# Splits moved to VectorE, block sums kept in PSUM, and a planned distance ahead of matmuls, in a planner-ordered attention and MoE kernel

## The chip, the cores and the metric

The kernel runs on one core of one Trainium2 chip. The metric is the device time of the whole program in microseconds, from one launch. Every engine (TensorE, VectorE, ScalarE, GpSimd, and SyncE, which issues the DMAs) works through its own list of instructions in the order in which the program wrote them, and waits on semaphores where an instruction needs another engine's result.

## What is computed

Attention over 16 heads (2 batches of 8, 768 rows of 64 numbers), in which a query sees only the keys of its own hash bucket, and two feed-forward stages behind it:

```python
mask = q_bucket[:, :, :, None] == k_bucket[:, :, None, :]
scores = np.where(mask, scale * np.matmul(q, k.transpose(0, 1, 3, 2)), -1e9)
attn = softmax(scores)
x = np.matmul(attn, v)          # as 1536 tokens of 512
...
h = x @ w_in                    # 512 -> 2048
x = (h / (1 + np.exp(-h))) @ w_out
...
a, b = x @ w1, x @ w2           # 512 -> 1024 each
out = ((a * b) @ w3) @ w_out
```

## The kernel before

**The planner.** The program's order isn't written by hand. Each step is an `op` with the engines that could do it and its cost in ns on each, the ops it needs, a due time, and the buffers it takes and gives back. `Plan.run` walks a modelled clock: an op is ready when the ops it needs have ended by its costs, each engine takes the op that could start soonest, and among equals the one due first. The order so found is the order of the instructions on each engine. On the chip only the order counts, not the modelled time. The costs are `dve(n)`, `act(n)`, `pool1(n)`, `pool2(n)`, plus a `TAIL` for each engine. A VectorE op with `port=True` is never planned beside a GpSimd op.

**Split numbers.** Matmuls run on rounded fp32 (`F32R`). So that nothing is lost, each operand is held as a high part (rounded, a copy) and a low part (`sub`, L251: the value less its high part), and each product is three matmuls: high by high, high by low, low by high. Whoever makes a new operand therefore makes two instructions, one copy and one subtraction.

**Stages.** Attention runs from 0 to about 325 us of the trace, in 96 units of 128 query rows: scores (L615), their maximum, exp, transposes (L655), a split of the transposed weights (`pth` on ScalarE, `ptl` on VectorE), and products with V (L688). `move` takes a group's result out of PSUM with two copies. Beside it the two last weight matrices are multiplied into one (L751). Behind it come the two feed-forward stages in cells: (1, c, ...) is chunk c of the first, (2, c, ...) of the second, each a rise (L913, L1020), a gate, and falls (L1064). A fall's PSUM result is added to `X` on VectorE (L1081).

**Weights.** `piece` brings in 128 by 1024 weights in two halves. The host passes them as 64-bit words. One half goes: DMA into one of three `raw` buffers (L273), two ScalarE (or GpSimd) reads (L290, L294 or L298), a join and a sign step on VectorE (L304, L309; the second frees `raw`), then the high part (`hi`, L248 on GpSimd) and the low part (`lo`). With `duo=True` four sums of the weight blocks are made on GpSimd (L373), and split too (`hi_sum`, `lo_sum`).

**Pair cells.** Two of the three token blocks are computed together as a 2 by 2 block product with seven block products instead of eight. `rise_pair` runs the `CHAIN` one, five, six, two, seven, four, three over three PSUM banks p, q, r. Bank p is added to in steps one, six, seven, four; between these steps ScalarE copies (`snap`) the intermediate value to an `sg` buffer, so that the first matmuls of six, seven and four wait for a copy. `plus` then adds a bank to such a copy on VectorE (L929) and gives the four blocks. `gated` or `gate`/`meet` make the activation from a block, and `rounded` splits it into `gh` and `gl`. The buffers `qraw`, `kraw`, `qhi`, `qlo`, `khi`, `klo` of the attention are lent to this stage as further `sg`, `gh` and `gl`. `split` and `less` (L853) split and subtract the blocks of X between the stages. PSUM has two banks `acc` and, behind the attention, six more, `more`.

## Time and profile before

| | |
|---|---|
| three runs | 776.03, 781.65, 782.9 us; median 781.65 us |
| profiled execution | 779.35 us |
| its span in the trace | 777.6 us, mean granted TensorE clock 0.986 |
| TensorE matmuls | busy 742.4 us, 95% |
| VectorE | busy 582.8 us, 75%, 1050 instructions |
| ScalarE | busy 440.9 us, 57%, 853 instructions |
| GpSimd | busy 466.7 us, 60%, 434 instructions |

The profiled execution is one of its own, and its span is 1.75 us shorter than its time. A busy share is a mean over stages with different limits, so the stages are read one by one. Busy times of matmuls overlap, so a busy TensorE may still be slower than its best; in the trace three matmuls of 512 columns in a row take 0.68 us.

### The profile page before, as it was taken

To read this page: it belongs to the slowest core of one execution; us is meant where nothing else is said; L and a number is where in the kernel's file an instruction comes from. 1 tells how busy PE (TensorE), PEld (TensorE's weight loads), DVE (VectorE), ACT (ScalarE), POOL (GpSimd) and SP (SyncE) were. 2 spreads that over 40 slices of the span, in tenths; PEclk is the share of its full clock that TensorE was granted. 3 is DMA by queue.
4 is the path that set the end of the run, shared out by engine and by line. 5 is a ranking of instruction groups with operands and counts; after the bars stand their busy time and mean duration, and the time that the engine had idled before them with its cause. 6 is when DMAs were issued, how large, how long until landed. Compare 5 with 4: busy or idle time off the path is not lost. (4 is left out here: it accounts for less than half of the span.)

```text
span 777.6 us, 11071 instructions
## 1 busy us (share of the span) xinstructions
PE 742.4 (95%) x3727; PEld 630.5 (81%) x3727; DVE 582.8 (75%) x1050; ACT 440.9 (57%) x853; POOL 466.7 (60%) x434
## 2 busy tenths in 40 slices
PE   6898999999999999899999998999999999999998
PEld 6887898989888989687788876878787788888886
DVE  4997899999999998694887788769568643745245
ACT  4778799787787777574655364524543544313110
POOL 3365988968675554627667576658495385827000
PEclk7999999999999999999999999999999999999999
DMA  7496868776564541400304223120301111200003
GB/s 206 134 228 167 217 149 207 188 193 167 146 177 110 163 120 38 133 1 28 102 7 136 80 83 101 35 82 19 117 1 36 59 41 54 83 1 0 1 14 149
DMA packets 27593, 77.25 MB, mean 99 GB/s; under 512 B 4424, under 2 KB 4520, under 8 KB 27536
## 3 DMA queue, kind: packets, MB, share of 16 engines
q1 hardware_dynamic: 27536, 76.55, 35.1%
q8 instruction: 29, 0.48, 0.3%
q14 instruction: 28, 0.23, 0.1%
HBM read 52.44 MB, written 5.29 MB: 74 GB/s over the span
## 5 line engine op out<-in xcount | busy, mean ns | idle before, releaser
L913 PE MATMUL more<-y,piece 128*128 128x512 f32 x504 | 135.6, 396 | 9.6 <-ACT sg L244 4.6
L913 PEld LDWEIGHTS more<-y,piece 128*128 128x128 f32 x504 | 94.8, 190 | 33.4 <-ACT sg L244 6.4
L251 DVE TENSOR_TENSOR ptl<-turn,pth 128x384 fp32r<-128x384 f32 x192 | 101.6, 548 | 11.8 <-ACT pth L244 10.8
L637 ACT ACTIVATE P<-score,st 128x768 f32<-128x768 f32 x96 | 95.4, 993 | 19.1 <-DVE st L631 18.8
L244 ACT ACTIVATE pth<-turn 128x384 fp32r<-128x384 f32 x192 | 88.1, 487 | 26.7 <-PE turn L655 26.2
L621 DVE TENSOR_REDUCE st<-score 128x1 f32<-128x768 f32 x96 | 90.8, 948 | 10.2 <-PE score L615 9.7
L655 PE MATMUL turn<-ident,P 128*128 128x128 f32 x576 | 87.5, 277 | 5.9 <-DVE ptl L251 5.4
L655 PEld LDWEIGHTS turn<-ident,P 128*128 128x128 f32 x576 | 68.4, 141 | 21.5 <-DVE ptl L251 14.0
L1081 DVE SCALAR_TENSOR_TENSOR X<-more,X 128x512 f32<-128x512 f32 x87 | 58.2, 685 | 25.4 <-PE more L1064 25.3
L251 POOL TENSOR_TENSOR piece<-x,piece 128x512 fp32r<-128x512 f32 x52 | 72.4, 1395 | 2.5 <-ACT piece L244 1.3
L688 PE MATMUL acc<-pth,V 128*128 128x384 f32 x192 | 67.7, 353 | 0.4 <-ACT pth L244 0.4
L688 PE MATMUL acc<-ptl,V 128*128 128x384 f32 x192 | 64.8, 338 | 0.2 <-DVE ptl L251 0.2
L248 POOL TENSOR_SCALAR piece<-x 128x512 fp32r<-128x512 f32 x50 | 36.5, 734 | 46.1 <-PE acc L1064 17.7
L1064 PE MATMUL more<-gh,piece 128*128 128x512 f32 x170 | 63.3, 389 | 0.0
L703 POOL TENSOR_TENSOR X<-X,xt 64x384 f32<-64x384 f32 x32 | 33.1, 1034 | 46.5 <-DVE X L246 22.0
L615 PE MATMUL score<-ka,qa 128*128 128x384 f32 x192 | 55.3, 369 | 3.8 <-ACT P L637 3.5
L294 ACT ACTIVATE t<-raw 128x512 uint32<-128x512 uint32 x49 | 32.9, 674 | 43.7 <-DVE x L309 10.2
L751 PE MATMUL acc<-piece,piece 128*128 128x512 f32 x192 | 55.2, 407 | 0.0
L1020 PE MATMUL more<-xh,piece 128*128 128x512 f32 x160 | 51.2, 389 | 0.0
L251 POOL TENSOR_TENSOR piece<-sum,piece 128x512 fp32r<-128x512 f32 x30 | 43.4, 1457 | 12.9 <-ACT piece L244 12.2
L615 PE MATMUL score<-kb,qb 76*128 76x384 f32 x192 | 50.0, 342 | 0.0
L244 ACT ACTIVATE sg<-more 128x512 f32<-128x512 f32 x28 | 16.7, 596 | 47.8 <-PE more L913 44.8
(225 smaller groups left out, 1859.5 us busy)
## 6 DMA issues: line engine op xcount, KB each, us to landing
raw<-in_w SPq DMA_DIRECT2D x32, 512.0 KB
raw<-in_wo SPq DMA_DIRECT2D x24, 512.0 KB
raw<-in_win SPq DMA_DIRECT2D x16, 512.0 KB
ka<-khi SPq DMA_DIRECT2D x30, 192.0 KB
qraw<-in_qT SPq DMA_DIRECT2D x8, 384.0 KB
kraw<-in_kT SPq DMA_DIRECT2D x8, 384.0 KB
vraw<-in_v SPq DMA_DIRECT2D x8, 384.0 KB
invb<-inverse SPq DMA_DIRECT2D x16, 192.0 KB
```

What stands on the lines that cost most here:

```text
L244: nc.scalar.activation(out=dst, in_=src, func=AF.Copy, scale=by)
L251: engine[e].tensor_tensor(out=dst, in0=src, in1=hi.bitcast(F32), op=ALU.subtract)
L615: nc.tensor.matmul(out=sc[:, g, :HF], lhsT=lhs[:k, qs], rhs=rhs[:k, g * HF:g * HF + HF], start=(k == 128), stop=(k != 128),)
L621: nc.vector.tensor_reduce(out=plan[uk("st")][:, 0:1], in_=plan[uk("S")][:, :, :HF], op=ALU.max, axis=AX.XY, negate=True)
L637: nc.scalar.activation(out=plan[uk("P")], in_=plan[uk("S")][:, :, :HF], func=AF.Exp, scale=s[:, 1:2], bias=s[:, 2:3], accum_out=plan[hk("s ...
L655: nc.tensor.transpose(pt[:, c * 128:c * 128 + 128], P[:, g, c * 128:c * 128 + 128], ident)
L688: nc.tensor.matmul(out=xo[:, :N], lhsT=V[:, c, :], rhs=plan[gk(x)][:, c, :], start=(c == 0 and x == "pth"), stop=(c == NQ - 1 and x == "ptl"),
L751: nc.tensor.matmul(out=plan[key + ("ps",)], lhsT=w[:, a, k], rhs=r[:, c], start=(k == 0 and n == 0), stop=(k == 7 and n == 2),)
L913: nc.tensor.matmul(out=plan[bk[b]], lhsT=w[:, a], rhs=y, start=(opens and j == 0 and m == 0), stop=(j == 1 and m == 2), skip_group_check=True)
L1020: nc.tensor.matmul(out=plan[key], lhsT=w[:, a], rhs=x, start=(k == 0 and n == 0), stop=(k == 3 and n == 2))
L1064: nc.tensor.matmul(out=plan[key], lhsT=a, rhs=x, start=(f == 0 and n == 0), stop=(f == 1 and n == 2))
L1081: nc.vector.scalar_tensor_tensor(out=dst, in0=plan[key], scalar=by, in1=dst, op0=ALU.mult, op1=ALU.add)
```

## The change

It has three parts.

- **Engines.** For weights needed later than 20 us before the planned end of the attention (`behind`), the low part is made on VectorE alone and the high part on ScalarE or GpSimd; until now both were GpSimd's. The low parts of the weight sums, of X (`split`), of the activations (`rounded`), and the differences `less` and the product `meet` are VectorE's alone; until now GpSimd could take them.
- **Block sums.** `plus` writes some sums back to the PSUM bank they came from (`back`), frees the `sg` copy instead of the bank, and the gate reads the bank. In stage 1 these are the blocks of q and r, in stage 2 that of r.
- **Planner.** An op of ScalarE, VectorE or GpSimd that a matmul waits for counts as ended 250 ns later, and from 325 us of the planned clock on 1000 ns later (`SLACK`, `SLACK_FFN`). The costs of `move` and `invert` are raised.

The instruction counts that follow: VectorE has 111 such steps more and 12 copies fewer, GpSimd 151 instructions fewer, ScalarE 42 high parts of weights and 12 copies more. TensorE has the same matmuls.

```diff
+SLACK, SLACK_FFN, FFN_AT = 250.0, 1000.0, 325.0
...
-                h.ready = max(h.ready, at + ns if e == "PE" and "PE" in h.on else o.end)
+                late = (SLACK if at < 1000.0 * FFN_AT else SLACK_FFN) if e in ("ACT", "DVE", "POOL") and "PE" in h.on else 0.0
+                h.ready = max(h.ready, at + ns if e == "PE" and "PE" in h.on else o.end + late)
...
-            soon = need < BEGIN + SOON
-            h = op({"POOL": pool1(STEP), "ACT": act(STEP)} if soon else {"POOL": pool1(STEP)}, hi, [j, opener], due + 3, take=first)
+            soon, behind = need < BEGIN + SOON, need >= T_END - 20
+            h = op({"POOL": pool1(STEP), "ACT": act(STEP)} if soon or behind else {"POOL": pool1(STEP)}, hi, [j, opener], due + 3, take=first)
...
-            done.append(op({"POOL": pool2(STEP), "DVE": dve(STEP)} if soon else {"POOL": pool2(STEP)}, lo, [h], due + 4,
+            done.append(op({"DVE": dve(STEP)} if behind else {"POOL": pool2(STEP), "DVE": dve(STEP)} if soon else {"POOL": pool2(STEP)}, lo, [h], due + 4,
...
-            more_done.append(op({"POOL": pool2(STEP)}, lo_sum, [h], due + 1.5 + n / 1e3, give=[tmp + (n,)], port=True))
+            more_done.append(op({"DVE": dve(STEP)}, lo_sum, [h], due + 1.5 + n / 1e3, give=[tmp + (n,)], port=True))
...
-                mv = op({"ACT": 2 * act(N), "DVE": 2 * dve(N)}, move, [xo], tu + 3.5, [("xt", gk("xt"))], [gk("xo")])
+                mv = op({"ACT": 1005, "DVE": 1050}, move, [xo], tu + 3.5, [("xt", gk("xt"))], [gk("xo")])
...
-            iv = op({"DVE": 250}, invert, exps, te + 3)
+            iv = op({"DVE": 430}, invert, exps, te + 3)
...
-        return op({"DVE": dve(BLK), "POOL": pool2(BLK)}, low, [a], due + 0.5, port=True)
+        return op({"DVE": dve(BLK)}, low, [a], due + 0.5, port=True)
...
-            return op({"DVE": dve(BLK), "POOL": pool2(BLK)}, fold, deps, due, port=True)
+            return op({"DVE": dve(BLK)}, fold, deps, due, port=True)
...
-    def rise_pair(key, bank, of, due):
+    def rise_pair(key, bank, of, due, back):
...
-            def plus(dst, src, after, give=()):
+            def plus(dst, src, after, give=(), back=False):
...
-                    nc.vector.tensor_tensor(out=plan[u[dst]], in0=plan[bk[src]], in1=plan[u[dst]], op=ALU.add)
+                    nc.vector.tensor_tensor(out=plan[bk[src] if back else u[dst]], in0=plan[bk[src]], in1=plan[u[dst]], op=ALU.add)
...
-                return op({"DVE": dve(BLK)}, add, after, d, give=give)
+                return op({"DVE": dve(BLK)}, add, after, d, give=[u[dst]] if back else give)
...
-                c11 = plus("x", "q", [last, marks["x"]], freed("q"))
+                c11 = plus("x", "q", [last, marks["x"]], freed("q"), back == 2)
...
-                c12 = plus("y", "r", [last, marks["y"]], freed("r"))
+                c12 = plus("y", "r", [last, marks["y"]], freed("r"), True)
...
-        return u, bk["p"], (c11, c12, c21, c22)
+        return u, bk, (c11, c12, c21, c22)
...
-        return op({"DVE": dve(BLK), "POOL": pool2(BLK)}, lambda e: sub(e, plan[gl], plan[src], plan[gh]),
+        return op({"DVE": dve(BLK)}, lambda e: sub(e, plan[gl], plan[src], plan[gh]),
...
-    def gated(key, src, deps, due, free=()):
+    def gated(key, src, deps, due, free=(), port=False):
...
-        g = op({"DVE": dve(BLK)}, gate, [a], due + 0.7, give=[src, *free])
+        g = op({"DVE": dve(BLK)}, gate, [a], due + 0.7, give=[src, *free], port=port)
...
-                u, p, (c11, c12, c21, c22) = rise_pair(cell + (f,), bank, of, start)
-                free = [p + ("token",)]
+                u, bk, (c11, c12, c21, c22) = rise_pair(cell + (f,), bank, of, start, 2 if part == 1 else 1)
+                p, r = bk["p"], bk["r"]
+                free, free_r = [p + ("token",)], [r + ("token",)]
...
-                    halves[0, 1] = gated(cell + (0, 1), u["x"], [c11], d - 3)
-                    halves[1, 2] = gated(cell + (1, 2), u["z"], [c22], d - 1)
+                    halves[0, 1] = gated(cell + (0, 1), bk["q"], [c11], d - 3, [bk["q"] + ("token",)])
+                    halves[1, 2] = gated(cell + (1, 2), u["z"], [c22], d - 1, port=True)
...
-                    halves[0, 2] = gated(cell + (0, 2), u["y"], [c12], d + 1)
+                    halves[0, 2] = gated(cell + (0, 2), r, [c12], d + 1, free_r)
...
-                    def meet(e, u=u):
-                        engine[e].tensor_tensor(out=plan[u["y"]], in0=plan[u["y"]], in1=plan[u["z"]], op=ALU.mult)
+                    def meet(e, u=u, r=r):
+                        nc.vector.tensor_tensor(out=plan[u["z"]], in0=plan[r], in1=plan[u["z"]], op=ALU.mult)
...
-                    g = op({"DVE": dve(BLK), "POOL": pool2(BLK)}, meet, [c12, c22], d + 1, give=[u["z"]], port=True)
-                    halves[f, 2] = rounded(cell + (f, 2), g, u["y"], d + 1)
+                    g = op({"DVE": dve(BLK)}, meet, [c12, c22], d + 1, give=[r, *free_r])
+                    halves[f, 2] = rounded(cell + (f, 2), g, u["z"], d + 1)
```

Lines below the planner move down by one to three: L251 is L253, L913 is L915, L1064 is L1067, L1081 is L1084 in the changed kernel.

The first place is TensorE in the fifth of the seven pair cells of stage 1, from the end of step five (`y_10`) to step six (`y_4`, into the bank of step one). Before:

```order
L913 MATMUL more_3572<-y_10_3535,piece_87 128x512
L913 MATMUL more_3572<-y_10_3549,piece_87 128x512
L913 MATMUL more_3572<-y_10_3535,piece_87 128x512
L913 MATMUL more_3571<-y_4_3529,piece_87 128x512
L913 MATMUL more_3571<-y_4_3543,piece_87 128x512
L913 MATMUL more_3571<-y_4_3529,piece_87 128x512
L1064 MATMUL more_3576<-khi_114,piece_86 128x512
```

Now:

```order
L915 MATMUL more_3578<-y_10_3539,piece_87 128x512
L915 MATMUL more_3578<-y_10_3553,piece_87 128x512
L915 MATMUL more_3578<-y_10_3539,piece_87 128x512
L1067 MATMUL acc_82<-khi_114,piece_86 128x512
L1067 MATMUL acc_82<-klo_115,piece_86 128x512
L1067 MATMUL acc_82<-khi_114,piece_86 128x512
L915 MATMUL more_3575<-y_4_3533,piece_87 128x512
L915 MATMUL more_3575<-y_4_3547,piece_87 128x512
L915 MATMUL more_3575<-y_4_3533,piece_87 128x512
```

Three matmuls of a fall now stand between five and six. Step one ends six matmuls ahead of six's first in the old order and nine ahead in the new one.

The second place is ScalarE at the same cell, up to the copy that step six waits for (`sg` from bank `more_0`). `raw` are weights just loaded, and a wait named DMAHW is one for a load. Before:

```order
L294 ACTIVATE t_0_95<-raw_1_91 128x512 [waits DVE_49]
L294 ACTIVATE t_1_96<-raw_2_92 128x512 [waits DMAHW7_49,DVE_49]
L290 ACTIVATE xm_0_3567<-raw_2_92 128x512 [waits Pool_49]
L294 ACTIVATE t_0_95<-raw_0_90 128x512 [waits DMAHW0_49,DVE_49]
L244 ACTIVATE sg_2_3555<-more_0_3571 128x512 [waits PE_49,Activation_49]
```

Now:

```order
L292 ACTIVATE x_0_93<-raw_2_92 128x512 [waits DMAHW7_49,DVE_49]
L246 ACTIVATE piece_5_88<-sum_1_3562 128x512
L246 ACTIVATE piece_6_89<-x_1_94 128x512 [waits DVE_49]
L296 ACTIVATE t_1_96<-raw_2_92 128x512
L246 ACTIVATE sg_2_3559<-more_0_3575 128x512 [waits PE_49]
L292 ACTIVATE x_1_94<-raw_0_90 128x512 [waits DMAHW0_49,DVE_49]
```

The last wait for a load stood directly ahead of the copy; now the next one stands behind it, and the nearest ahead is four rows up. A high part of a weight (`piece` from `x`) that waits for VectorE stands between.

The third place is VectorE, at the weight steps of that cell (t, x and xm are the join and sign steps, X the falls' sums). Before:

```order
L304 SCALAR_TENSOR_TENSOR t_0_95<-x_0_93,t_0_95 128x512
L304 SCALAR_TENSOR_TENSOR t_1_96<-x_1_94,t_1_96 128x512
L1081 SCALAR_TENSOR_TENSOR X_74<-acc_1_82,X_74 128x512 [waits PE_49]
L309 SCALAR_TENSOR_TENSOR x_0_93<-raw_2_92,t_0_95 128x512 [waits DMAHW6_49,DVE_49,Pool_49]
L1081 SCALAR_TENSOR_TENSOR X_74<-more_5_3576,X_74 128x512 [waits PE_49]
L251 TENSOR_TENSOR gl_1_3565<-sg_2_3555,gh_1_3562 128x512 [waits Activation_49]
L309 SCALAR_TENSOR_TENSOR x_1_94<-raw_0_90,t_1_96 128x512 [waits DMAHW7_49,DVE_49,Pool_49]
L304 SCALAR_TENSOR_TENSOR t_0_95<-xm_0_3567,t_0_95 128x512 [waits Activation_49]
L309 SCALAR_TENSOR_TENSOR xm_0_3567<-raw_1_91,t_0_95 128x512 [waits DMAHW0_49,DVE_49]
L304 SCALAR_TENSOR_TENSOR t_1_96<-xm_0_3567,t_1_96 128x512 [waits Activation_49]
L1081 SCALAR_TENSOR_TENSOR X_74<-more_4_3575,X_74 128x512 [waits PE_49]
L309 SCALAR_TENSOR_TENSOR xm_0_3567<-raw_2_92,t_1_96 128x512 [waits DMAHW1_49,DVE_49]
```

Now:

```order
L306 SCALAR_TENSOR_TENSOR t_1_96<-x_1_94,t_1_96 128x512
L253 TENSOR_TENSOR piece_5_88<-sum_1_3562,piece_5_88 128x512 [waits Activation_49]
L311 SCALAR_TENSOR_TENSOR x_1_94<-raw_0_90,t_1_96 128x512 [waits DMAHW5_49,DVE_49]
L306 SCALAR_TENSOR_TENSOR t_0_95<-xm_0_3571,t_0_95 128x512
L253 TENSOR_TENSOR piece_6_89<-x_1_94,piece_6_89 128x512 [waits Activation_49]
L311 SCALAR_TENSOR_TENSOR xm_0_3571<-raw_1_91,t_0_95 128x512 [waits DMAHW6_49,DVE_49]
L306 SCALAR_TENSOR_TENSOR t_1_96<-x_0_93,t_1_96 128x512 [waits Activation_49]
L311 SCALAR_TENSOR_TENSOR x_0_93<-raw_2_92,t_1_96 128x512 [waits DMAHW7_49,DVE_49]
L306 SCALAR_TENSOR_TENSOR t_0_95<-x_1_94,t_0_95 128x512 [waits Activation_49,Pool_49]
L311 SCALAR_TENSOR_TENSOR x_1_94<-raw_0_90,t_0_95 128x512 [waits DMAHW0_49,DVE_49]
L1084 SCALAR_TENSOR_TENSOR X_74<-acc_1_82,X_74 128x512 [waits PE_49]
L931 TENSOR_TENSOR more_4_3579<-more_4_3579,sg_2_3559 128x512 [waits PE_49]
```

The sign steps that free `raw` stood between sums that wait for TensorE. Now low parts of weights stand between them, with waits for ScalarE, and the sums come behind; the last row writes a block sum back to its bank.

## Rows read from the trace of the kernel before

**Rows 1.** Windows by stretch: us, busy us and instructions per engine, granted clock, DMA

```profile
0.00:297.00 297.00, 280.06 (x1700) 252.53 (x1701) 264.73 (x600) 234.90 (x490) 200.16 (x195) 0.98 0.65 168
20.00:100.00 80.00, 72.06 (x468) 64.47 (x467) 70.66 (x157) 64.67 (x132) 49.40 (x46) 0.99 0.74 187
100.00:297.00 197.00, 194.01 (x1177) 175.46 (x1176) 184.56 (x424) 161.01 (x343) 144.77 (x136) 1.00 0.61 156
297.00:777.60 480.60, 462.33 (x2029) 378.01 (x2027) 318.02 (x451) 205.98 (x364) 266.53 (x240) 0.99 0.17 57
400.00:550.00 150.00, 143.60 (x621) 116.81 (x620) 116.19 (x154) 64.77 (x112) 100.44 (x91) 0.99 0.24 78
```

**Rows 2.** Timeline of TensorE at its waits behind the attention: start, us, group, [idle before]

```profile
328.03 0.50 PE L1064 MATMUL acc<-qhi,piece 128*128 128x512 f32 x1 [2.29 <-ACT X L244]
...
367.84 3.01 PE L913 MATMUL more<-y,piece 128*128 128x512 f32 x12 [1.13 <-ACT qraw L244]
...
383.72 0.96 PE L913 MATMUL more<-y,piece 128*128 128x512 f32 x3 [1.31 <-ACT sg L244]
...
447.42 0.96 PE L913 MATMUL more<-y,piece 128*128 128x512 f32 x3 [0.45 <-ACT kraw L244]
...
459.35 0.96 PE L913 MATMUL more<-y,piece 128*128 128x512 f32 x3 [0.76 <-DVE sg L929]
...
482.57 1.65 PE L913 MATMUL more<-y,piece 128*128 128x512 f32 x3 [2.52 <-ACT sg L244]
...
516.81 0.97 PE L913 MATMUL acc<-y,piece 128*128 128x512 f32 x3 [1.15 <-ACT sg L244]
...
549.85 0.96 PE L913 MATMUL more<-y,piece 128*128 128x512 f32 x3 [1.45 <-ACT kraw L244]
```

**Rows 3.** Chain that ended last, 477 to 489 us: start, us, what

```profile
477.14 0.57 DVE x L309
...
477.76 3.52 DMA raw<-in_wo
...
481.93 0.59 ACT sg L244
...
488.46 0.68 PE more L913 x3
```

**Rows 4.** Windows of four us behind three waits

```profile
328.00:332.00 4.00, 3.97 (x11) 3.16 (x12) 0.28 (x1) 2.20 (x4) 3.73 (x3) 0.60 0.41 135
484.00:488.00 4.00, 4.00 (x15) 3.21 (x14) 2.06 (x3) 1.28 (x2) 3.90 (x5) 0.77 0.39 131
518.00:522.00 4.00, 4.00 (x20) 3.28 (x19) 0.91 (x3) 1.18 (x2) 2.24 (x3) 1.00 0.26 69
```

**Rows 5.** Groups by line and form, whole run: count, busy us, mean ns, idle before

```profile
L251 POOL TENSOR_TENSOR piece<-sum,piece 128x512 fp32r<-128x512 f32 x30 | 43.4, 1457 | 12.9 <-ACT piece L244 12.2 <-POOL piece L248 0.7
...
L251 DVE TENSOR_TENSOR gl<-sg,gh 128x512 fp32r<-128x512 f32 x18 | 18.3, 1025 | 7.3 <-ACT gh L244 7.3
...
L244 ACT ACTIVATE piece<-sum 128x512 fp32r<-128x512 f32 x27 | 16.7, 623 | 6.3 <-POOL sum L373 2.5 <-PE more L913 1.9 <-PE acc L1064 1.9
...
L929 DVE TENSOR_TENSOR sg<-more,sg 128x512 f32<-128x512 f32 x23 | 15.8, 689 | 26.0 <-ACT sg L244 14.0 <-PE more L913 12.0
...
L246 DVE COPY X<-acc 64x384 f32<-64x384 f32 x22 | 12.2, 555 | 0.3
...
L853 DVE TENSOR_TENSOR X<-X 128x512 f32<-128x512 f32 x16 | 10.8, 695 | 0.0
...
L251 DVE TENSOR_TENSOR piece<-x,piece 128x512 fp32r<-128x512 f32 x4 | 2.8, 688 | 1.2 <-ACT piece L244 1.2
```

**Rows 6.** Waits, whole run: us in total, times, longest

```profile
POOL piece L248 <- DVE x L309: 16.8, 9, 4.2
...
POOL piece L248 <- DVE xm L309: 15.5, 7, 4.8
...
PE turn L655 <- DVE ptl L251: 5.4, 9, 1.3
```

## Prediction

> **What bounds the kernel now.** I read the busy shares by stretch first, then the waits of TensorE, then the chain of work that ended last, and only then the costs of single groups.
>
> TensorE is the bound nearly everywhere: busy 462.33 of the 480.60 us behind the attention and 194.01 of 197.00 us in its later part [rows 1]. No change here takes a matmul away, so all there is to gain is its idle time and the time at a lowered clock: 18.3 us behind the attention, 3.0 us in the later attention, 7.9 us from 20 to 100 us, and 6.0 us in the first 20 us (297.00 - 280.06 - 7.94 - 2.99), which the change leaves in their order. The other engines count only where TensorE waits for them.
>
> Behind the attention the reader should look at where TensorE stands still [rows 2]. Five of the eight waits shown have one place: twelve matmuls of a pair cell (steps one and five) have run, and the three of step six wait for ScalarE's copy out of bank p (383.72, 447.42, 482.57, 516.81, 549.85 us: 1.31, 0.45, 2.52, 1.15, 1.45, together 6.88 us). Two more, 1.13 and 0.76 us, wait for a ScalarE copy and a VectorE sum. The 2.29 us at 328 us stand where the attention hands over.
>
> Why the copy is late is seen in the chain [rows 3]. VectorE's sign step frees a raw weight buffer at 477.71 us; the load into it takes 3.52 us; ScalarE's read of it stands in its queue directly ahead of the copy, which so starts at 481.93 us, and TensorE goes on at 482.57. The copy itself needs 0.59 us. The wait is thus set by VectorE being late with a weight step, handed on through a load and through ScalarE's fixed order.
>
> A long wait costs a second time. After the 2.29 us the granted clock over the next four us is 0.60 of 2.4 GHz, after the 2.52 us it is 0.77, both a mixture with the lower level of 1.2 GHz; after the 1.15 us it is 1.00 [rows 4]. By these rows the two drops cost 4 x 0.40 = 1.6 and 4 x 0.23 = 0.9 us.
>
> **Part 1: the planned distance.** Between the last matmul of one and the first of six (and of seven and four) the new order puts three more matmuls, 0.68 us [rows 3]. Counted through the whole order, 25 of these 30 returns to bank p had six matmuls between; now none has fewer than nine. Each of the five waits shrinks by up to 0.68 us if the copy ends when it did: 4 x 0.68 + 0.45 = 3.2 us. Of the other 3.7 us I take half, 1.9 us, since in the cells two to seven, where the wait for a load stood directly ahead of that copy on ScalarE all six times, it does so in one now, and in the others two rows up or more. Below 1.9 us no drop of the clock is seen here, so 0.9 us come back as well. Sum 5.9 us. Bounds: 0 if ScalarE's copies come later by as much, 7.8 us if all five waits and the drop vanish.
>
> For the 1.13 and 0.76 us [rows 2] the same distance of one us is planned; I take 1.0 of 1.9 us, bounds 0 and 1.9. The hand-over at 328 us I leave at nothing: in both orders the first fall stands right behind the attention's last products, and a planned distance has nothing to put between. Bounds there: 3.9 us gained (the wait and its clock), 3 us lost by a second wait of that kind, since the third fall now returns to a bank of the first one.
>
> **Part 2: low parts on VectorE.** 111 steps move, and GpSimd loses them at 1457 ns each [rows 5], 162 us of its 266.5 us behind the attention [rows 1]. On VectorE such a step takes 688 ns where GpSimd doesn't read beside it, and 1025 ns in the group in which it often does [rows 5]. I take the 688, since GpSimd has a good third of its work left: 76 us more, to 394 of 480.6 us, 82%. What hides them is VectorE's idle time behind the attention, 162.6 us [rows 1]. ScalarE gets 42 high parts at 623 ns [rows 5], 26 us, to 232 us, 48%. None of this lies on TensorE's path by itself, so the term is 0. If that cover is gone, it is the rival below.
>
> The moved steps have a new kind of wait. GpSimd's high part waited for VectorE's sign step 16 times, 2.0 us on average, at most 4.8 us [rows 6], and nobody stood behind it. Now ScalarE can wait in its place, with copies out of PSUM queued behind it. Against that, VectorE's low parts need only the high part, and the sign steps, which freed the raw buffers too late, stand closer together and no longer between sums that wait for TensorE. I set the two against each other and count neither; as a bound, 16 waits beyond the 1.40 us that a distance of 2.04 us leaves (the copy starts 0.64 us before TensorE goes on [rows 3]) are 16 x 0.6 = 9.6 us.
>
> SBUF to SBUF against PSUM: the 22 sums written back cost nothing by the rows, 689 ns for a sum that reads PSUM and 695 ns for one all in SBUF [rows 5]; a write into PSUM isn't in the trace, bounds -0.1 and +0.35 us each (the spread 688 to 1025), all on VectorE. The banks q and r are held for the gate's two steps longer, about 1.3 us (623 + 689 ns), which the order has already spread over its eight banks. The Trainium skill, Perfetto Trace Analysis, section Optimizing Scalar/DVE Operations, gives VectorE about 125 ns of access time on PSUM against about 60 on SBUF. By that the 22 sums would cost an estimated 22 x 65 ns = 1.4 us of VectorE time; the rows show no such difference on reads.
>
> **Part 3: the attention.** Twelve copies of 555 ns [rows 5] leave VectorE for ScalarE, 6.7 us. From 20 to 100 us VectorE is busy 70.66 of 80 us and TensorE idle 7.9 us [rows 1], and in the whole run TensorE waits 5.4 us in nine places for VectorE's low part of the transposed weights [rows 6]. That stretch holds about a quarter of the copies, 1.8 us, and 250 ns of distance go ahead of each such wait. I take 1.5 us. Bounds: 6 us gained of the 7.9, 4 us lost where another order of the same tight stretch falls badly.
>
> **Sum.** 5.9 + 1.0 + 0 + 0 + 1.5 = 8.4 us, from 779.35 to 771.0 us. The profiled execution lies 2.3 us below the median of 781.65 us, so against that it would be 1.4% less, against its own time 1.1%. The three runs before spread over 6.9 us, so about 1% (7.8 us) is what a measurement here can tell from no change: faster by over 1% of the median is below 773.8 us, slower above 789.5 us.
>
> **Rivals.**
>
> *The loads still decide (small gain).* The change doesn't touch raw buffers or loads, and 17 of 53 copies out of PSUM now have a wait for a load in the row directly ahead on ScalarE, against 13. Then the distance alone counts, 3.2 us, and the attention's order gives nothing: 776 us. For it speaks that the chain goes through the load [rows 3]; against it that the copy ahead of step six has mostly lost that neighbour.
>
> *VectorE becomes the bound (slower).* Place: 400 to 550 us, where VectorE is busy 116.2 of 150 us [rows 1]. The 111 steps spread evenly over some 440 us, so 38 fall there. At 688 ns that is 142 us, at 1025 ns [rows 5] 155 us, 5.2 us more than there is; it decides from (150 - 116.2) / 38 = 0.89 us a step. The sign steps behind them come late as well, so the 16 waits that ScalarE took over reach TensorE at 9.6 us (part 2). Less the 3.2 us of the distance that is 11.6 us lost: 791 us. For it: the low part already took 1025 ns on average, and it reads two operands in SBUF, as GpSimd's remaining steps do. Against: that mean was taken beside a GpSimd with 111 more steps. The Trainium skill, SBUF — State Buffer, section Who interferes with whom, states that a VectorE instruction with two SBUF inputs contends with a GpSimd instruction that reads SBUF, whichever starts second standing still for the whole of the other. That would be the mechanism of the 1025 ns, and the rows 688 and 1025 agree with it.
>
> *Everything overlaps (larger gain).* All of part 1, the two waits, and most of the attention's idle time go: 7.8 + 1.9 + 6 = 15.7 us: 764 us. It needs every late load to be gone as well.
>
> **How the numbers follow.** Forecast 771 (766 to 775): 0.47. Small gain, 776: 0.29. VectorE as the bound, 791: 0.12. Larger gain, 764: 0.12. Faster by over 1%: the larger gain, 0.38 of the forecast and a little of the rest, 0.51. Slower by over 1%: most of the third case and a little that I don't see, 0.12. Within 1%: 0.37. The range runs from 762 to 784 us: it takes in the first, second and fourth case with the spread of the runs, and leaves out the slow one.
>
> **What would show it.** Right: the waits for the copy ahead of step six under 0.8 us each and the clock at 1.00 behind them; VectorE some 380 to 400 us busy behind the attention and its low parts near 690 ns; GpSimd near 105 us there; no wait of TensorE over 2 us between 340 and 600 us. Wrong: low parts near 900 ns or more, falls' sums behind them with TensorE waiting for X; ScalarE waiting for the sign step with a copy behind it; or the time lost in the attention, whose order of steps changes from about 20 us on.

## The result, and the profile after

The changed kernel takes 770.56 us (median of 7 runs, 769.55 to 772.76), the kernel before 780.13 us (median of 7 runs, 776.03 to 785.45). The ratio is 0.9882, 95% interval 0.9843 to 0.9921: faster by a little over 1%. The forecast was 771.0 us. The profiled execution spans 768.8 us, 8.8 us less than before.

I read the windows by stretch first, as for [rows 1]. They hold us, busy us and instructions of TensorE, its weight loads, VectorE, ScalarE and GpSimd, then the granted clock and the DMA share. The changed kernel:

```profile
20.00:100.00 80.00, 74.43 (x487) 67.46 (x486) 71.63 (x162) 69.04 (x143) 55.99 (x52) 1.00 0.76 197
100.00:297.00 197.00, 189.08 (x1145) 170.49 (x1144) 173.32 (x406) 164.03 (x349) 128.14 (x118) 1.00 0.59 151
297.00:360.00 63.00, 56.02 (x263) 46.47 (x262) 54.00 (x86) 37.71 (x76) 25.73 (x23) 0.95 0.19 61
360.00:600.00 240.00, 239.59 (x1055) 197.43 (x1054) 208.40 (x331) 129.28 (x229) 48.11 (x54) 1.00 0.21 69
400.00:550.00 150.00, 150.00 (x663) 124.05 (x662) 128.69 (x203) 71.39 (x126) 31.30 (x37) 1.00 0.25 80
297.00:768.80 471.80, 458.98 (x2033) 378.23 (x2031) 359.74 (x563) 221.85 (x398) 93.24 (x102) 0.99 0.18 59
```

Two stretches of the kernel before that its own rows didn't cut this way:

```profile
297.00:360.00 63.00, 59.37 (x284) 49.27 (x283) 50.26 (x84) 39.65 (x78) 29.64 (x27) 0.97 0.20 62
360.00:600.00 240.00, 230.54 (x998) 187.34 (x997) 179.19 (x243) 111.86 (x194) 162.56 (x149) 0.99 0.19 64
```

From 360 to 600 us TensorE is busy 239.59 of 240 us instead of 230.54, and from 400 to 550 us all of the time [rows 1]. That is where the gain lies, and it is more than the whole of it: 9.1 us of idle time are gone, and the granted clock is 1.00 there against 0.99. Elsewhere time was lost on the whole. From 20 to 100 us TensorE's idle time fell from 7.9 to 5.6 us, but in the later attention it rose from 3.0 to 7.9 us [rows 1], and at the hand-over, 297 to 360 us, from 3.6 to 7.0 us at a lower clock (0.95 against 0.97). In the first 20 us the granted clock was 1.00 against 0.78 before. Kernel 8 below, with the same order on TensorE, had 0.83 there, so this lies in the execution and not in the change. Even so the attention's last product with V began at 328.51 us against 325.40. VectorE has 41.7 us more to do behind the attention (359.74 against 318.02), GpSimd 173 us less (93.24 against 266.53).

TensorE's waits, in its timeline (start, us, group, idle before and what ended it), the changed kernel, at the hand-over:

```profile
314.39 1.54 PE L657 MATMUL turn<-ident,P 128*128 128x128 f32 x6 [2.06 <-DVE ptl L253]
...
330.09 0.50 PE L1067 MATMUL acc<-qhi,piece 128*128 128x512 f32 x1 [1.24 <-DVE kraw L970]
...
336.93 1.66 PE L1023 MATMUL more<-y,piece 128*128 128x512 f32 x6 [0.27 <-DVE y L253]
340.90 5.42 PE L1023 MATMUL more<-y,piece 128*128 128x512 f32 x15 [2.31 <-DVE y L253]
```

and from 590 to 604 us:

```profile
593.43 1.62 PE L915 MATMUL more<-y,piece 128*128 128x512 f32 x6 [0.27 <-DVE X L1084]
...
602.96 0.73 PE L1067 MATMUL more<-piece,gh 128*128 128x512 f32 x2 [1.33 <-DVE qraw L931]
```

All seven waits of [rows 2] from 367 to 550 us are gone, the five ahead of step six among them. From 350 us to the end the two rows above and one of 0.35 us at 643 us are the only ones over 0.2 us. The hand-over has kept a wait of 1.24 us where it had 2.29 us [rows 2], and has got two new ones: 2.06 us at 314.39 us, where the attention's last units wait for VectorE's low part of the transposed weights, and 2.31 us at 340.90 us.

The groups by line and form of the whole run (count, busy us, mean ns, idle before), the changed kernel, answer to [rows 5]:

```profile
L253 DVE TENSOR_TENSOR y<-X,y 128x512 fp32r<-128x512 f32 x30 | 23.5, 822 | 7.3 <-ACT y L246 7.3
L253 DVE TENSOR_TENSOR piece<-x,piece 128x512 fp32r<-128x512 f32 x33 | 23.3, 715 | 1.6 <-ACT piece L246 1.2
L311 DVE SCALAR_TENSOR_TENSOR x<-raw,t 128x512 uint32<-128x512 uint32 x33 | 23.2, 708 | 0.3
...
L253 DVE TENSOR_TENSOR piece<-sum,piece 128x512 fp32r<-128x512 f32 x30 | 20.8, 693 | 1.1 <-ACT piece L246 1.1
...
L253 DVE TENSOR_TENSOR gl<-sg,gh 128x512 fp32r<-128x512 f32 x28 | 19.9, 718 | 6.0 <-ACT gh L246 5.8
...
L931 DVE TENSOR_TENSOR more<-more,sg 128x512 f32<-128x512 f32 x12 | 8.3, 693 | 1.7 <-PE more L915 1.7
```

The low parts of weights and weight sums on VectorE take 693 to 715 ns, as taken; gl<-sg, which took 1025 ns [rows 5], takes 718. Those of X, y<-X, have a mean of 822 ns; that comes from the hand-over, and kernel 10 has 737. The sums that write into PSUM take 693 ns.

The waits over the whole run (us, times, longest), the changed kernel, answer to [rows 6]:

```profile
ACT piece L246 <- DVE x L311: 16.1, 8, 4.0
...
PE turn L657 <- DVE ptl L253: 9.1, 13, 2.1
```

ScalarE has taken over GpSimd's wait for the sign step, eight times, but the chains that lead to TensorE's three waits behind 350 us don't contain it. The attention's own wait has grown from 5.4 to 9.1 us.

### The profile page after: what moved, and what is told of

Same layout as the page of the kernel before. It is cut to its first block, busy times and chain, and to the rows that moved or that the text cites. A ratio compares the mean times of both kernels' runs of the same rounds, so it can differ in the third digit from the quotient of the medians.

```text
span 768.8 us, 11042 instructions
## 1 busy us (share of the span) xinstructions
PE 737.5 (96%) x3727; PEld 629.5 (82%) x3727; DVE 615.6 (80%) x1149; ACT 464.5 (60%) x905; POOL 283.2 (37%) x283
## 4 chain that ended last, share of the span: by engine, by line
PE 67%; DVE 19%; DMA 5%; ACT 5%; issue 2%; POOL 1%; ACTq 0%; DVEq 0%; SPq 0%; POOLq 0%
PE more L1067 16%; PE more L915 12%; PE more L1023 6%; PE acc L690 6%; PE score L617 5%; PE turn L657 5%; PE acc L753 5%; PE acc L1067 4%; PE acc L915 4%; DMA raw<-in_w 4%; DVE ptl L253 4%; DVE st L623 3%; PE acc L1023 3%; DVE y L253 2%; PE acc L506 1%
## 5 line engine op out<-in xcount | busy, mean ns | idle before, releaser
L253 DVE TENSOR_TENSOR ptl<-turn,pth 128x384 fp32r<-128x384 f32 x192 | 102.9, 549 | 15.9 <-ACT pth L246 15.3
L915 PE MATMUL more<-y,piece 128*128 128x512 f32 x444 | 114.8, 390 | 0.8 <-ACT sg L246 0.3
L915 PEld LDWEIGHTS more<-y,piece 128*128 128x128 f32 x444 | 83.1, 188 | 19.2 <-ACT sg L246 0.8
L657 PE MATMUL turn<-ident,P 128*128 128x128 f32 x576 | 89.1, 277 | 9.7 <-DVE ptl L253 9.1
L300 POOL TENSOR_SCALAR t<-raw 128x512 uint32<-128x512 uint32 x26 | 20.2, 778 | 165.8 <-DMA raw<-in_w 59.4
L1084 DVE SCALAR_TENSOR_TENSOR X<-more,X 128x512 f32<-128x512 f32 x98 | 66.1, 685 | 17.4 <-PE more L1067 17.0
L1067 PE MATMUL more<-gh,piece 128*128 128x512 f32 x178 | 65.0, 389 | 0.0
L705 POOL TENSOR_TENSOR X<-X,xt 64x384 f32<-64x384 f32 x32 | 33.1, 1033 | 46.8 <-DVE X L248 36.8
L915 PE MATMUL acc<-y,piece 128*128 128x512 f32 x186 | 48.5, 390 | 0.0
L296 ACT ACTIVATE t<-raw 128x512 uint32<-128x512 uint32 x46 | 30.9, 671 | 26.8 <-DMA raw<-in_w 17.3
L915 PEld LDWEIGHTS acc<-y,piece 128*128 128x128 f32 x186 | 34.8, 188 | 7.6 <-ACT sg L246 0.3
L1067 PEld LDWEIGHTS more<-gh,piece 128*128 128x128 f32 x178 | 33.4, 188 | 6.9
```

The costliest lines, as they stand in the source:

```text
L253: engine[e].tensor_tensor(out=dst, in0=src, in1=hi.bitcast(F32), op=ALU.subtract)
L657: nc.tensor.transpose(pt[:, c * 128:c * 128 + 128], P[:, g, c * 128:c * 128 + 128], ident)
L915: nc.tensor.matmul(out=plan[bk[b]], lhsT=w[:, a], rhs=y, start=(opens and j == 0 and m == 0), stop=(j == 1 and m == 2), skip_group_check=True)
L1067: nc.tensor.matmul(out=plan[key], lhsT=a, rhs=x, start=(f == 0 and n == 0), stop=(f == 1 and n == 2))
L1084: nc.vector.scalar_tensor_tensor(out=dst, in0=plan[key], scalar=by, in1=dst, op0=ALU.mult, op1=ALU.add)
```

## The experiments

Each kernel ran beside the kernel before on one chip: 1 to 4 on one, 5, 6, 8 and 10 on a second, 7, 9 and 11 on a third, 12 on a fourth. Between these groups the ratios compare better than the times. "TensorE" and "GpSimd" are busy us in the window 360 to 600 us of the profiled execution. A wait that stands near 600 us can fall inside that window in one kernel and behind it in another: the 1.33 us at 602.96 us of the changed kernel stand at 600.12 us in kernel 10, nearly all inside.

| kernel | median us | ratio to before, 95% interval | TensorE | GpSimd |
|---|---|---|---|---|
| before | 780.13 | | 230.54 | 162.56 |
| changed | 770.56 | 0.9882 (0.9843 to 0.9921) | 239.59 | 48.11 |
| 1 changed, no distance | 772.87 | 0.9897 (0.9849 to 0.9945) | 237.88 | 46.84 |
| 2 before, distance alone | 784.27 | 1.0046 (1.0015 to 1.0078) | 234.25 | 176.44 |
| 3 changed, no distance in the attention | 770.75 | 0.9877 (0.9835 to 0.9919) | 238.96 | 45.13 |
| 4 changed, sums in SBUF | 771.65 | 0.9894 (0.9858 to 0.9929) | 238.44 | 44.22 |
| 5 changed, weights' low parts on GpSimd | 768.04 | 0.9851 (0.9789 to 0.9914) | 239.69 | 119.33 |
| 6 before, weights' low parts alone | 768.34 | 0.9858 (0.9802 to 0.9914) | 237.97 | 79.16 |
| 7 before, other moves alone | 775.08 | 0.9946 (0.9916 to 0.9975) | 234.61 | 136.39 |
| 8 changed, GpSimd kept busy, 3 additions | 784.23 | 1.0060 (1.0032 to 1.0088) | 231.77 | 128.48 |
| 9 the same, 1 addition | 773.53 | 0.9937 (0.9913 to 0.9961) | 237.28 | 72.78 |
| 10 changed, sums behind the splits | 768.69 | 0.9856 (0.9801 to 0.9911) | 237.59 | 47.81 |
| 11 kernel 6, sums behind the splits | 767.45 | 0.9846 (0.9821 to 0.9872) | 237.12 | 80.35 |
| 12 kernel 11, distance behind the attention | 764.84 | 0.9779 (0.9731 to 0.9826) | 238.11 | 87.03 |

### Kernels 1 to 3: is it the distance?

The prediction gave 5.9 of its 8.4 us to the distance. Kernel 1 takes it out of the changed kernel:

```diff
-SLACK, SLACK_FFN, FFN_AT = 250.0, 1000.0, 325.0
+SLACK, SLACK_FFN, FFN_AT = 0.0, 0.0, 325.0
```

> The changed kernel with both planned distances set to 0; low parts stay on VectorE and the sums in PSUM. Theory D (the distance removes TensorE's waits for the copies of the pair cells): six matmuls stand ahead of step six again, waits for the copy of some 5 us in total come back from 360 to 600 us, time 776 to 780 us. Rival L (moving the low parts off GpSimd made VectorE punctual, so that loads and copies come in time): waits stay away, VectorE's low parts near 0.70 us, time 769 to 773 us.

Kernel 2 puts the three lines of the distance (the constants, and the two lines that add them to the time from which a matmul may be placed) into the kernel before, and nothing else.

> The kernel before with only the two planned distances added (250 and 1000 ns); low parts of weights stay on GpSimd, sums in SBUF. Theory D: waits for the copies mostly gone, time 769 to 773 us. Rival L: low parts of VectorE stay near 1.0 us, loads come as late as before, waits shrink by 0.68 us each, about 3 us in all: 776 to 778 us.

Kernel 3 keeps the distance behind the attention only (`SLACK` 0, `SLACK_FFN` 1000).

> The changed kernel with the 250 ns of the attention set to 0, the 1000 ns behind it kept. Theory A (the 250 ns spread the attention's steps so that TensorE waits more for VectorE's low part of the transposed weights): the first 297 us lose less idle time, time 767 to 769 us. Rival: the attention's idle time comes from its order by chance or from VectorE's load, time 770 to 773 us.

Without any distance the changed kernel keeps nearly all of its gain, as rival L had it. Ten of the fifteen returns from step one to six, and all from seven to four, stand six matmuls apart again in its order, as before, yet of the waits ahead of step six one is back in TensorE's timeline:

```profile
389.20 0.96 PE L915 MATMUL more<-y,piece 128*128 128x512 f32 x3 [1.54 <-ACT sg L246]
```

With the distance alone TensorE is busy 3.7 us more from 360 to 600 us, close to the 3.2 us of the sum, but long waits stay, and the attention loses more than that; 784 us is beyond both of its theories. Windows of kernel 2:

```profile
0.00:297.00 297.00, 273.53 (x1616) 246.38 (x1617) 253.25 (x562) 226.04 (x471) 194.90 (x189) 0.95 0.66 166
100.00:297.00 197.00, 189.48 (x1122) 170.94 (x1121) 170.97 (x399) 156.71 (x333) 139.66 (x130) 0.97 0.63 159
360.00:600.00 240.00, 234.25 (x1024) 191.08 (x1023) 184.81 (x236) 112.77 (x197) 176.44 (x160) 1.00 0.20 66
```

Its later attention is idle 7.5 us at a clock of 0.97 (before: 3.0 us and 1.00 [rows 1]), in a profiled execution that is one of its slower ones (786.99 us). The last product with V begins 13.2 us later than before, at 338.63 us, and what follows takes 446.6 us against 452.2. So behind the attention the distance does help by itself; no run has it there alone in the kernel before. Why a long wait stays is seen in its chain that ended last, 450 to 461 us (start, us, what):

```profile
454.11 0.69 DVE xm L311
...
454.87 0.62 POOL piece L250
455.49 1.13 POOL sum L375
456.62 1.26 POOL piece L253
...
457.91 0.67 ACT xm L292
...
459.69 0.52 ACT piece L246
460.21 0.49 ACT qraw L246
```

VectorE's sign step is followed by three of GpSimd's steps (a high part, a sum, a low part of 1.26 us); the last frees a weight buffer; three steps of ScalarE wait for that, and the copy out of the bank, fourth in ScalarE's fixed order, starts at 460.21 us. A matmul farther away can't hide a copy that is late by more than the distance. The theory that the distance makes the gain of the changed kernel falls with kernel 1. Kernel 3 is not to be told from the changed kernel: the distance within the attention is worth nothing there.

### Kernel 4: the sums written back to PSUM

```diff
-                c11 = plus("x", "q", [last, marks["x"]], freed("q"), back == 2)
+                c11 = plus("x", "q", [last, marks["x"]], freed("q"))
...
-                c12 = plus("y", "r", [last, marks["y"]], freed("r"), True)
+                c12 = plus("y", "r", [last, marks["y"]], freed("r"))
```

and the gates read the sums from SBUF again.

> The changed kernel with the block sums left in their SBUF copies, as before the change; all else kept. Theory: writing back to PSUM costs and gives nothing (0.69 us either way), time 769 to 773 us. Rival: freeing the SBUF copies early, or reading the gate from PSUM without using the shared side with GpSimd, is what keeps VectorE punctual: sums and gates take 0.8 us or more, waits come back, 774 us or more.

771.65 us against 770.56: no difference beyond the spread. Writing into PSUM costs nothing that can be seen (693 ns a sum), and gives nothing.

### Kernels 5 to 7: which half of the move?

Kernel 5 is the changed kernel with the low parts of weights and weight sums on GpSimd again:

```diff
-            done.append(op({"DVE": dve(STEP)} if behind else {"POOL": pool2(STEP), "DVE": dve(STEP)} if soon else {"POOL": pool2(STEP)}, lo, [h], due + 4,
+            done.append(op({"POOL": pool2(STEP), "DVE": dve(STEP)} if soon else {"POOL": pool2(STEP)}, lo, [h], due + 4,
...
-            more_done.append(op({"DVE": dve(STEP)}, lo_sum, [h], due + 1.5 + n / 1e3, give=[tmp + (n,)], port=True))
+            more_done.append(op({"POOL": pool2(STEP)}, lo_sum, [h], due + 1.5 + n / 1e3, give=[tmp + (n,)], port=True))
```

> The changed kernel with the low parts of the weights and of the weight sums back on GpSimd, behind the attention too; the added distances, the other steps that are fixed to VectorE (splits of X, low parts of the gated values, their products) and the sums in PSUM stay. Theory L (GpSimd's chain of about 1.45 us a low part was what made TensorE wait from 360 us on): the waits for the copy ahead of step six and others come back in part, TensorE is busy 234 to 236 us of 360 to 600 us as with the distances alone, 775 to 780 us. Rival M (it is the other moved steps that count, the low parts of the gated values and the products on VectorE alone): no waits from 360 us on, 239 us busy there, 769 to 773 us. Rival D (the distances carry the gain): fell with the kernel without distances; it too would give 769 to 773 us.

Kernel 6 is the kernel before with these two lines as the change has them (and the high parts shared with ScalarE there), and nothing else.

> The kernel before with one part of the change only: the low parts of the weights and of the weight sums on VectorE behind the attention, and their high parts on ScalarE or GpSimd there. No added distance, the block sums in SBUF, the splits of X shared by VectorE and GpSimd as before. Theory L: most of the gain comes with this alone, TensorE busy 237 to 239 us of 360 to 600 us, 771 to 775 us. Rival (the part needs the distances, or the other moved steps): waits ahead of step six stay, 230 to 234 us busy, 777 to 781 us.

Kernel 7 is the kernel before with the other half alone: splits of X, low parts of gated values, Q and K, and products on VectorE alone.

```diff
-        return op({"DVE": dve(BLK), "POOL": pool2(BLK)}, low, [a], due + 0.5, port=True)
+        return op({"DVE": dve(BLK)}, low, [a], due + 0.5, port=True)
```

and the same in the three other places where the change has it.

> The kernel before with the other half of the moves only: the low parts of X, of the gated values, of Q and K, and the products of block sums on VectorE alone; the low parts of the weights and of the weight sums stay on GpSimd. No added distance, sums in SBUF. Theory G (what made TensorE wait is that GpSimd, busy 163 of 240 us from 360 to 600 us, hands on the steps of a weight late, so that ScalarE and VectorE stand behind them with the copies; any half of the moves that brings GpSimd to about 120 us or less is enough): at most one or two waits there, TensorE busy 237 to 240 us, 768 to 773 us. Rival W (it is the shorter chain of a weight alone that counts): GpSimd's low parts still take 1.45 us, waits ahead of step six stay, busy 230 to 234 us, 777 to 782 us. Rival D (that the half of it that was enough together with the distances needs them): 773 to 778 us.

Theory L fell with kernel 5, whose time lies 1 us under rival M's range: the weights' low parts stand on GpSimd at their old price, and TensorE has no wait of 0.2 us or more from 360 us until one of 0.66 us that ends at 600.35 us. GpSimd's groups of kernel 5, whole run:

```profile
L253 POOL TENSOR_TENSOR piece<-sum,piece 128x512 fp32r<-128x512 f32 x30 | 43.5, 1456 | 44.7 <-ACT piece L246 41.2 <-issue 3.2
```

It stood idle 44.7 us ahead of these 30 steps, waiting for ScalarE's high parts; in the kernel before it was 12.9 us [rows 5]. GpSimd waits there for others where others had waited for it; that its slow step in the chain so does no harm is argued from this row. Kernel 6, the other half without any distance, gets the whole gain too (768.34 us). Kernel 7 gets less: 775.08 us, between theory G and rival W and inside the range of rival D, that this half needs the distance. Its longest waits for ScalarE's copies from 360 to 580 us are 0.51 and 0.94 us, but it waits 3.07 us at the hand-over and 3.08 us at 594 us. Windows of the kernel before, kernel 6 and kernel 7:

```profile
360.00:580.00 220.00, 211.00 (x913) 171.47 (x912) 161.17 (x216) 102.88 (x180) 151.29 (x138) 0.99 0.20 67
```

```profile
360.00:580.00 220.00, 217.97 (x960) 179.65 (x959) 177.88 (x273) 119.09 (x212) 77.27 (x73) 1.00 0.23 72
```

```profile
360.00:580.00 220.00, 218.29 (x957) 178.93 (x956) 175.83 (x244) 106.67 (x185) 131.03 (x124) 1.00 0.22 70
```

So each half alone removes most of the waits from 360 to 580 us, 7.0 and 7.3 of 9.0 us, and they don't add: the second half finds little left there. What kernel 7 lacks against kernel 5 lies at the hand-over and at 594 us. The two differ by the distance, the sums in PSUM, the planner's costs for the attention, and the high parts shared with ScalarE; which of these counts there was not tried, so rival D is open. Nor was the low part tried without the high part in kernel 6.

### Kernels 8 and 9: GpSimd kept busy

The changed kernel, the order of TensorE, VectorE and ScalarE unchanged, with idle additions on GpSimd ahead of each moved low part behind the attention (their result is not used). Kernel 8 has three, kernel 9 one:

```diff
+    def occupy():
+        if spare:
+            for _ in range(3):
+                nc.gpsimd.tensor_tensor(out=spare[0], in0=ident, in1=ident, op=ALU.add)
...
             def lo(e, value=value, c=c):
+                occupy()
                 sub(e, plan[name][:, 1, c], value(), plan[name][:, 0, c])
```

> The changed kernel in its own order on TensorE, VectorE and ScalarE; GpSimd alone gets three idle additions of 128 x 128 in SBUF ahead of each low part of a weight or weight sum that VectorE makes behind the attention, so that it is about as busy there as in the kernel before. Their result is not used. Theory P (GpSimd's work beside VectorE's makes VectorE's two-input steps in SBUF longer, as seen at the hand-over, 1.14 against 0.61 us): the low parts of weights go from about 0.71 to 0.9 to 1.1 us, VectorE gets 25 to 40 us more work behind the attention, and waits come back: 775 to 781 us. Theory L without P (it counts only that GpSimd's slow step no longer stands in the chain of a weight): low parts stay near 0.72 us, 769 to 773 us.

> The run with three idle additions on GpSimd ahead of each moved low part (784.2 us) with one addition in place of three; order of all other steps the same. Theory G (additions hurt by the time that they hold up GpSimd's next step of a weight, 0.6 us each): 0.6 us of delay is within what the plan leaves free at most steps; a part of the waits comes back, 770 to 776 us. Theory P (they hurt by making VectorE's steps longer): low parts of weights stay a third as much longer, 0.72 to 0.73 us against 0.71 and 0.76, and the time is a third of the way, 773 to 776 us, with VectorE's share of its span as in the run with three.

With three additions the whole gain is gone, with one 3.0 us of it (by the ratios 4.3). Theory L without P, which had 769 to 773 us for kernel 8, falls. Theory P falls too: 784 us is beyond its 775 to 781, and the rise of the low parts that it needs didn't come. Groups of kernel 8 from 360 to 600 us, on GpSimd and on VectorE:

```profile
L267 POOL TENSOR_TENSOR spare<-ident 128x128 bf16<-128x128 f32 x141 | 82.0, 582 | 9.8
```

```profile
L313 DVE SCALAR_TENSOR_TENSOR t<-x,t 128x512 uint32<-128x512 uint32 x18 | 14.2, 794 | 5.6 <-POOL t L307 3.9 <-ACT t L303 1.5 <-ACT x L299 0.3
...
L253 DVE TENSOR_TENSOR piece<-sum,piece 128x512 fp32r<-128x512 f32 x18 | 13.6, 758 | 7.7 <-ACT piece L246 6.7 <-POOL piece L250 1.0
L253 DVE TENSOR_TENSOR piece<-x,piece 128x512 fp32r<-128x512 f32 x18 | 13.0, 724 | 1.0 <-ACT piece L246 0.7
```

The low parts take 724 to 762 ns, not 900 to 1100; VectorE has 632.2 us to do in the whole run against 615.6. The chain of kernel 8 from 392 to 428 us, its shares by line, shows where the rest comes from; in the changed kernel the same stretch of the chain is the second fence, TensorE alone:

```profile
by line: POOL spare L267 24.2%; POOL sum L383 14.7%; DVE X L1094 14.6%; POOL t L307 7.9%; DVE gl L253 6.9%; DVE sg L980 6.6%; issue 5.3%; DVE t L313 4.7%; DVE piece L253 4.0%; DVE x L318 3.6%; ACT piece L246 3.6%; DVE kraw L980 3.5%; POOL p
```

```profile
by line: PE more L1067 45.3%; PE acc L915 17.9%; PE more L1023 15.1%; PE more L915 14.5%; PE acc L1067 7.6%
```

GpSimd's sums and shifts of a weight (L383, L307) come late behind the additions (L267), 46.8% of the chain together. From 360 to 600 us ScalarE waits 4.9 us for those sums where it waited 0.9 us in the changed kernel, and TensorE waits for ScalarE's copies again, 0.95 us at 401.81 us and 1.19 us at 426.17 us. How the loss divides between GpSimd's lateness and the 16.6 us more on VectorE these two runs don't settle: kernel 9's 773.53 us fits both of its theories.

### Kernels 10 and 11: the hand-over

At 340.90 us TensorE waits for VectorE's low parts of X. VectorE and GpSimd there, in the timelines of the changed kernel:

```profile
336.18 9.09 DVE L253 TENSOR_TENSOR y<-X,y 128x512 fp32r<-128x512 f32 x8 [6.14 <-ACT y L246]
```

```profile
334.98 3.04 POOL L365 TENSOR_TENSOR sum<-piece 128x512 f32<-128x512 f32 x2
338.10 1.05 POOL L375 TENSOR_TENSOR sum<-sum,sum 128x256 f32<-128x256 f32 x1
339.12 1.17 POOL L375 TENSOR_TENSOR sum<-sum 128x256 f32<-128x256 f32 x1
340.26 1.18 POOL L375 TENSOR_TENSOR sum<-sum,sum 128x256 f32<-128x256 f32 x1
```

Eight low parts take 9.09 us, 1.14 us each, while GpSimd sums weights beside them. In the kernel before GpSimd ended a sum at 332.38 us and stood idle until 346.33 us, and the same eight took 4.89 us from 333.46 us on. Kernel 10 lets the second of each pair of GpSimd's sums begin with a copy of one column of the last low part of X, so that it waits:

```diff
-                def again(e, x=x, c=c):
+                def again(e, x=x, c=c, n=n):
                     p = plan[name].bitcast(F32)
+                    if n:
+                        nc.gpsimd.tensor_copy(out=plan[x][:, :1], in_=lows[-1][:, :1].bitcast(F32))
                     nc.gpsimd.tensor_tensor(out=plan[x], in0=p[:, 0, c], in1=p[:, 1, c], op=ALU.add)
...
+            lows.append(dst(1))
```

> The changed kernel with one order added on GpSimd: of each pair of weight sums that it forms, the second begins with a copy of one column of the last low part of X that VectorE has made by then in the program, so that GpSimd's sums at the hand-over from the attention (from 334 us on) wait until VectorE's splits of X are through. Theory H (at the hand-over VectorE's low parts of X take 1.14 us instead of about 0.6 us because GpSimd sums beside them): the row of eight low parts falls to 0.6 to 0.7 us each, the wait of 2.3 us at 341 us and most of the lower clock behind it go, 766 to 769 us. Rival (VectorE is late there for its own order, or the sums now come late and the first steps of the next cell wait): the wait at 341 us stays or comes back a few us later, 770 to 773 us.

Kernel 11 is the same edit in kernel 6.

> The kernel before with only the low parts of weights and weight sums on VectorE behind the attention, as in the run of that part alone (768.3 us), and with the order of GpSimd's sums behind VectorE's splits of X that took 2.3 us off the hand-over in the changed kernel. Theory H and G together: the wait of 2.5 us at 337 us and the lower clock behind it (1.2 us) go, the rest as in that run: 764 to 767 us. Rival (X's splits are shared here, so GpSimd's own half of them stands behind VectorE's and keeps TensorE waiting): a wait at 337 us or a few us later stays, 768 to 771 us.

VectorE in kernel 10, and TensorE behind it:

```profile
335.47 4.91 DVE L253 TENSOR_TENSOR y<-X,y 128x512 fp32r<-128x512 f32 x8 [6.10 <-ACT y L246]
```

```profile
336.22 9.35 PE L1028 MATMUL more<-y,piece 128*128 128x512 f32 x38 [0.27 <-DVE y L253]
```

The eight take 4.91 us, and TensorE runs 38 matmuls without a stop where it had waited 2.31 us. The cause at this place is shown. In kernel 11 less goes: the wait of 2.51 us at 337 us becomes one of 0.89 us, and one of 1.1 us ahead of it stays, now put down to GpSimd's sum. On the time of the whole kernel the edit gives 1.9 us (768.69 against 770.56 us) and 0.9 us on kernel 6, less than the spread of the runs.

### Kernel 12: what is left for the distance

Kernel 11 with `SLACK` 0 and `SLACK_FFN` 1000, as in kernel 3.

> The kernel before with the low parts of weights and weight sums on VectorE behind the attention, the order of GpSimd's sums behind VectorE's splits of X, and the planned distance behind the attention alone (none within it); durations that the planner holds for the attention's steps stay as in the kernel before. That is the run with the sums behind the splits (767.5 us) plus the distance. Theory (distances and moved low parts pay for the same waits, and little is left: waits of 0.8, 1.2 and 0.7 us ahead of step six at 361, 381 and 414 us): these three go, 763 to 766 us. Rival (the distance moves steps of TensorE and VectorE that other places feel, as the distances alone made the kernel slower): new waits elsewhere, 767 to 771 us.

764.84 us, ratio 0.9779: the fastest of all, 5.7 us under the changed kernel, on another chip (8.0 us by the ratios). Kernel 11's waits at 361, 381 and 414 us (0.80, 1.19, 0.65 us) have become one, at 418 us; new ones of about 1 us stand at 591 and 601 us. The intervals of the ratios of kernels 11 and 12 just overlap (0.9821 and 0.9826), so that the last 2 to 3 us, which its theory had, are likely but not certain. The profiled execution of kernel 12 is the slowest of its six (769.42 us), so the trace doesn't show where they come from.

## Why the prediction was right, and where it was not

The time is right by luck, the account of it is not: a gain given to the wrong part, a gain as large left out, and losses at the hand-over and in the attention cancel. Of the signs of being right, the waits ahead of step six, the clock behind them, the low parts near 690 ns and GpSimd's load (93 us) came. VectorE's load (360 us, not 380 to 400) did not come, and a wait over 2 us stands behind 340 us (2.31 us at 340.90), where there was to be none.

**The distance (5.9 us, and 1.0 us for two other waits).** This is the step that failed: "Each of the five waits shrinks by up to 0.68 us". The price was right for the distance by itself, 3.2 us forecast and 3.7 us more TensorE work from 360 to 600 us in kernel 2, but it is not what removed the waits: all but one go without it (kernel 1), and with it alone waits of 5.8 us stay from 360 to 600 us, where the seven made 8.8 us (kernel 2). In the changed kernel it is worth 2.3 us by the medians and 1.2 by the ratios (kernel 1), less than the spread. The half of the remaining 3.7 us that I gave to the order of the copies had the right place, ScalarE's queue, and the wrong reason. The clock came back to 1.00 there, as forecast, with the waits. But "Below 1.9 us no drop of the clock is seen here" misreads the kernel before: behind waits of 0.65 and 0.75 us, at 609.97 and 611.45 us, its granted clock is 0.64, between the levels of 1.2 and 2.4 GHz. In the changed kernel it is 0.58 behind the wait at 340.90 us. Both in windows of four us:

```profile
611.00:615.00 4.00, 3.55 (x10) 2.81 (x11) 0.60 (x2) 2.98 (x7) 0.67 (x1) 0.64 0.46 131
```

```profile
341.00:345.00 4.00, 4.00 (x11) 2.80 (x12) 4.00 (x4) 1.38 (x3) 3.92 (x5) 0.58 0.00 0
```

**The low parts (0 us).** "None of this lies on TensorE's path by itself, so the term is 0" is the costly error. The chain [rows 3] had shown it: VectorE late with a weight's step, a load behind that, ScalarE's step behind the load, the copy behind ScalarE's step. Moving low parts takes load off GpSimd and makes VectorE's own steps shorter, so the whole chain of a weight runs earlier. That is read from the chains; the runs show its effect. Kernel 6, that one edit with the high parts that go with it, makes 11.8 us against the 780.15 us of the kernel before on its chip. I had read the cause of the lateness and then priced only a cure for its effect.

**VectorE's load.** Forecast 394 us behind the attention, measured 359.7. The 76 us of moved steps cost 41.7 us net, because steps that stayed became shorter with GpSimd quiet: x<-raw from 941 to 708 ns and gl<-sg from 1072 to 712 ns in the groups from 360 to 600 us. So the rival that VectorE becomes the bound did not come about: it needed 0.89 us a step, and the weights' and sums' low parts had 0.69 to 0.72. Its mechanism is real all the same, and decided one place.

**The hand-over (0 us).** I set a gain of 3.9 us against a loss of 3 us. TensorE's idle time rose by 3.4 us there and the clock fell. Two new waits make it. I looked for one in TensorE's order of banks; the one of 2.31 us came from GpSimd's sums, which the new order puts beside VectorE's splits (kernel 10). The one of 2.06 us at 314.39 us stands behind VectorE: its chain runs through a weight's low part (1.13 us) and one of Q (2.23 us), which VectorE makes ahead of the low part that TensorE waits for. Kernel 10 has it too (2.07 us). Kernel 5, where the weights' low parts are GpSimd's, and kernels 1 and 3, without the distance in the attention, have no wait for that low part there, but others (3.15 us at 330.20 us in kernel 5), so the cause of this one stays open. The Trainium skill, SBUF — State Buffer, section Who interferes with whom, has it that the second of two such instructions stands still for the whole of the first. Alone VectorE's step takes 0.61 us (4.91 us for eight in kernel 10) and GpSimd's sum of 128 x 256 takes 0.74 (737 ns, the mean of sum<-x,xm, its shortest group in the changed kernel); side by side they take 1.14 and about 1.17 us, so a pair needs a little less than the 1.35 us that taking turns would give. The trace agrees with the rule in kind, and nearly in size.

**The attention (1.5 us gained).** The early stretch gained 2.3 us, the later lost 4.9 us, net a loss of 2.6 us, within the bound of 4 us. Which edit does it was not tried alone. Kernels 1, 3 and 4 with the new durations of the planner for the attention's steps, and kernel 2 with the old ones and a distance there, are all idle 6.8 to 7.5 us from 100 to 297 us; kernels 6, 7, 11 and 12, with neither, 3.1 to 4.2 us. So either of the two seems enough to disturb that order; this is argued from the comparison, not shown.

**The write-back (0 us).** Right: kernel 4. A sum that writes to PSUM takes 693 ns, one that writes to SBUF 689 [rows 5]; the difference that the Trainium skill, Perfetto Trace Analysis, section Optimizing Scalar/DVE Operations, gives for the two memories isn't seen.

**The rival of the loads.** It held that the distance alone counts and loads go on deciding, 776 us. The distance counts least, and the loads no longer decide. But its mechanism has stayed: loads still stand in ScalarE's queue in the changed kernel, and one reaches TensorE directly, as a wait of 0.35 us at 643.04 us, by the chain of [rows 3] (start, us, what). The chain of the waits at 593 and 603 us passes another (3.71 us from 579.82 us on), with 18 us of VectorE's and ScalarE's steps behind it. At 643.04 us:

```profile
637.00 0.70 DVE x L311
...
637.84 3.92 DMA raw<-in_w
...
641.84 0.66 ACT t L296
642.50 0.50 ACT sg L246
...
643.04 1.20 PE more L915 x4
```

## What to carry to other kernels

When an engine waits for a copy, follow the copy's engine back through its fixed order to the step that is late, and price the removal of that lateness, not only the distance that hides it. An engine that is busy two thirds of a stretch can set the end if its steps stand in other engines' queues: taking part of its work away (kernel 6, and kernel 5 with the distance) was worth as much here as taking all of it, though another part without the distance (kernel 7) was worth about half. Where two engines slow each other, a move of work costs less than the moved steps' own time, but a planner that keeps the two apart in its plan did not keep them apart on the chip here; an order between them did (kernel 10).

## What was not expected of the hardware

The slowing at the hand-over is mutual: GpSimd's sums lose 0.43 us each by it, VectorE's steps 0.53. And small additions on GpSimd (128 x 128, mean 0.58 us) lengthen VectorE's low parts little, the weight sums' from 701 to 758 ns from 360 to 600 us: VectorE's t<-x took 794 ns beside them in kernel 8, and 930 ns in kernel 5, where GpSimd, no busier from 360 to 600 us, made low parts.
